# A fixed order by due times, w_in in four tiles, and weights loaded into lent places, in a convolution with two dense layers on one core

## The chip, the core and the metric

The kernel runs on one core of one Trainium2 chip. The engines of the core that matter here are TensorE (PE, matrix products), VectorE (DVE), ScalarE (ACT, one function of one input), GpSimd (POOL) and SyncE (SP), whose queue issues the DMAs. Each engine works off its own instructions in the order in which the program lists them; a semaphore makes one wait for another. The metric is the device time of one execution in microseconds (us), as the median of several runs.

## The reference

There are 8192 tokens of width 192 (two sequences of 4096).

```
w   = softmax(weight_gen)                       # [8192, 8 heads, 7 taps]
x   = sum over 7 taps of w * x shifted          # each head weighs its 24 columns
h   = x @ w_in                                  # 192 -> 2048
P   = a0 + a1 h + a2 h^2 + a3 h^3
Q   = 1 + |b0| |h| + |b1| h^2
y   = (P / (Q + 1e-6)) @ w_out                  # 2048 -> 192
xn  = y / sqrt(mean(y^2) + 1e-6) * rms_g
g   = xn @ w_gate ;  val = xn @ w_val           # 192 -> 1536
out = (g * sigmoid(g) * val) @ w_out2           # 1536 -> 192
```

## The kernel before

**Blocks.** The tokens go through in 32 blocks of 256. A block has four quarters of its 2048 hidden columns, numbered on through the program (block b has quarters 4b to 4b+3; below, .0 to .3 stand for the four of the block that a sentence is about). A step is a "job": a key, an engine, a cost, what it depends on and which places it takes.

The jobs of a block, with the lines of their instructions:
- convolution: `v` (POOL, L349), seven products of a shifted x with its weights; `a` (DVE L358, two reductions; POOL additions in the first blocks); `hl` (ACT L368) and `ll` (POOL L372) split the sum into two fp16 parts; `xt` transposes them by DMA (SP L377). `s` is the softmax in seven steps, of which `mx` (DVE L306) is the first.
- `mm1` of a quarter (PE L738): 20 matmuls into a place `h` in PSUM, of which there are two. So an mm1 waits until the quarter two before it has gone through its last reader, `d`.
- the rational function of a quarter, on tiles of 128x1024: `sq` (ACT L748) and `ab` (ACT L752), then `q` (DVE L755, the denominator), `ln` and `ex` (ACT L759, L762: one over it), `p1` and `p2` (DVE L766, L770: the numerator, in place in h), `hi` (DVE L775: the quotient in fp16, g1h), `qc` (ACT L778), `m` (POOL L781: denominator times g1h), `d` (DVE L784: what that leaves of the numerator) and `lo` (POOL L788: the low part, g1l).
- `mm2` (PE L804 to L806) into one PSUM place acc; `y`, `sj`, `rm` (ACT), the root `rn` (POOL L831 to L835, five small steps), `xs_` and `xh` (ACT L839, L843), `xl` (POOL L847, two instructions), `xnt` (SP L852: a transpose by DMA that gives xnT).
- `mm3` (PE L738 on gv): products with the gate and the value weights in two halves; `silu` (ACT), `prod` (DVE L883), `mm4` (PE L892) and the store.

**Weights.** They come as float64. An `ld` job loads a group of pieces as pairs of 32-bit words into a place `raw` (two of them) by SP. Three jobs decode it: `da` (ACT L409 to L412), `db` (DVE L431, L437, L440, L443: passes over the bits) and `dc` (ACT L455: squares and their sum). A list MODES gives each group its way of decoding: mode 0 has one pass more on DVE, mode 2 two instructions more on ACT per piece. From a maximum of the sums a scale is taken (`sc`), and `sa` and `sb` split each weight into a high and a low fp16 part (w1A, w1B, w1C for w_in; wo1h and wo1l for w_out; w3g.. and w3v.. for gate and value). The keys are in, o1, g, v and o2. The last pieces of w_in are copied to their place by DMA (L555).

**Order.** Before anything is emitted, a function `order()` simulates the engines and lists the jobs. Among the jobs of an engine whose inputs are ready it takes, at each moment of that simulation, the one that is due first. A job of block b is due at 4b times T_SLOT plus a number in a table OFF for its kind.

## Time and profile before

| | before |
|---|---|
| median of 3 runs | 1434.73 us (1432.48 to 1434.94) |
| profiled execution | 1432.05 us |
| its span in the profile | 1430.3 us |
| mean granted clock of PE | 0.957 of full speed |
| busy share of the span | PE 87%, DVE 82%, ACT 80%, POOL 73% |

All times of rows are of this one profiled execution. Its own time has 1.75 us outside the span. The profile's first part gives each engine's busy time over the whole span; a view by windows does so for stretches. A view of waits says for whom an engine stood idle, and for how long; a timeline lists single instructions with, in brackets, the idle time just ahead of one and what ended it.

### The profile page before, as it was taken

To read this page: it belongs to the slowest core of one execution; us is meant where nothing else is said; L and a number is where in the kernel's file an instruction comes from. 1 tells how busy PE (TensorE), PEld (TensorE's weight loads), DVE (VectorE), ACT (ScalarE), POOL (GpSimd) and SP (SyncE) were. 2 spreads that over 40 slices of the span, in tenths; PEclk is the share of its full clock that TensorE was granted. 3 is DMA by queue.
4 is the path that set the end of the run, shared out by engine and by line. 5 is a ranking of instruction groups with operands and counts; after the bars stand their busy time and mean duration, and the time that the engine had idled before them with its cause. 6 is when DMAs were issued, how large, how long until landed. Compare 5 with 4: busy or idle time off the path is not lost.

```text
span 1430.3 us, 26378 instructions
## 1 busy us (share of the span) xinstructions
PE 1240.0 (87%) x11026; PEld 1131.7 (79%) x11026; DVE 1174.0 (82%) x1021; ACT 1145.3 (80%) x1404; POOL 1041.2 (73%) x877
## 2 busy tenths in 40 slices
...
DMA packets 70376, 54.19 MB, mean 38 GB/s; under 512 B 54002, under 2 KB 65906, under 8 KB 69360
## 3 DMA queue, kind: packets, MB, share of 16 engines
...
q14 instruction: 34, 0.28, 0.1%
...
## 4 chain that ended last, share of the span: by engine, by line
PE 50%; POOL 17%; DVE 10%; ACT 10%; DMA 9%; issue 5%; SPq 0%; POOLq 0%; ACTq 0%; DVEq 0%
PE gv L738 19%; PE h L738 11%; PE acc L892 8%; POOL g1l L788 6%; DMA xnT<-xn 5%; PE acc L804 4%; PE acc L806 4%; PE acc L805 4%; POOL xn L847 4%; POOL tA L781 3%; DMA raw<-in_moe_w_in_dram 2%; DVE ac L358 2%; ACT L1285 1%; DVE tA L755 1%; DVE tA L784 1%
## 5 line engine op out<-in xcount | busy, mean ns | idle before, releaser
L781 POOL TENSOR_TENSOR tA<-tA,g1h 128x1024 f32<-128x1024 f32 x128 | 276.7, 2163 | 162.6 <-DVE g1h L775 146.7
L788 POOL TENSOR_TENSOR g1l<-tA,tC 128x1024 f16<-128x1024 f32 x128 | 305.7, 2400 | 105.4 <-DVE tA L784 62.8
L738 PE MATMUL h<-xt,w1A 128*128 128x256 f16 x1024 | 221.0, 279 | 78.0 <-DVE tA L784 76.5
L892 PE MATMUL acc<-wo,gp 128*128 128x192 f32 x1488 | 253.1, 326 | 0.6 <-ACT osb L898 0.5
L804 PE MATMUL acc<-wo1h,g1h 128*128 128x192 f16 x1024 | 251.9, 246 | 1.1 <-ACT y L811 1.1
L806 PE MATMUL acc<-wo1h,g1l 128*128 128x192 f16 x1024 | 251.9, 246 | 0.0
L805 PE MATMUL acc<-wo1l,g1h 128*128 128x192 f16 x1024 | 251.9, 246 | 0.0
L892 PEld LDWEIGHTS acc<-wo,gp 128*128 128x128 f32 x1488 | 240.3, 190 | 2.2 <-ACT osb L898 0.8
L349 POOL TENSOR_TENSOR pt<-xc,wg 128x384 f32<-128x384 f32 x224 | 240.3, 1089 | 1.0
L766 DVE SCALAR_TENSOR_TENSOR h<-tB,cf,h 128x1024 f32<-128x1024 f32 x128 | 164.0, 1281 | 87.0 <-ACT tA L752 87.0
L748 ACT ACTIVATE tB<-h 128x1024 f32<-128x1024 f32 x128 | 130.5, 1021 | 130.4 <-PE h L738 130.4
L784 DVE SCALAR_TENSOR_TENSOR tA<-h,cf,tA 128x1024 f32<-128x1024 f32 x128 | 164.0, 1281 | 63.0 <-POOL tA L781 62.9
L738 PE MATMUL h<-xt,w1C 128*128 128x256 f16 x1024 | 200.4, 278 | 0.0
L755 DVE SCALAR_TENSOR_TENSOR tA<-tB,cf,tA 128x1024 f32<-128x1024 f32 x128 | 188.4, 1472 | 0.5 <-ACT tB L748 0.4
L738 PEld LDWEIGHTS <-w1A 128*128 128x128 f16 x1024 | 102.2, 100 | 103.3 <-DVE tA L784 64.0
L738 PE MATMUL gv<-xnT,w3gA 128*128 128x256 f16 x756 | 157.2, 272 | 30.6 <-DMA xnT<-xn 30.5
L738 PE MATMUL gv<-xnT,w3vA 128*128 128x256 f16 x768 | 169.5, 273 | 3.3 <-ACT gp L878 3.3
L775 DVE SCALAR_TENSOR_TENSOR g1h<-h,cf,tC 128x1024 f16<-128x1024 f32 x128 | 163.7, 1279 | 8.6 <-ACT tC L762 3.4
L770 DVE SCALAR_TENSOR_TENSOR h<-tB,cf,h 128x1024 f32<-128x1024 f32 x128 | 163.6, 1278 | 0.0
L883 DVE SCALAR_TENSOR_TENSOR gp<-gp,val_s,gv 128x1536 f32<-128x1536 f32 x64 | 115.8, 1809 | 51.2 <-PE gv L738 51.2
L759 ACT ACTIVATE tC<-tA,cf 128x1024 f32<-128x1024 f32 x128 | 145.9, 1141 | 1.4 <-DVE tA L755 1.0
L762 ACT ACTIVATE tC<-tC,lnb 128x1024 f32<-128x1024 f32 x128 | 145.8, 1139 | 1.0
...
## 6 DMA issues: line engine op xcount, KB each, us to landing
...
```

What stands on the lines that cost most here:

```text
L349: nc.gpsimd.tensor_tensor(out=pt_t[b][:, k].rearrange("p i (h g) -> p i h g", h=NH), in0=xc_t[k0][:, o0 + k:o0 + k + 2, :].rearrange("p i ...
L738: nc.tensor.matmul(out=dst, lhsT=w[:, fs], rhs=xt[:, :, c, :], start=(n == 0), stop=(n == 4))
L755: nc.vector.scalar_tensor_tensor(out=tA[q], in0=tB[q], scalar=cfb(q)[:, 1:2], in1=tA[q], op0=ALU.mult, op1=ALU.add)
L766: nc.vector.scalar_tensor_tensor(out=h, in0=tB[q], scalar=cf[:, 4:5], in1=h, op0=ALU.add, op1=ALU.mult)
L775: nc.vector.scalar_tensor_tensor(out=g1h[q], in0=hps[q], scalar=cf[:, 3:4], in1=tC[q], op0=ALU.add, op1=ALU.mult)
L781: nc.gpsimd.tensor_tensor(out=tA[q], in0=tA[q], in1=g1h[q], op=ALU.mult)
L784: nc.vector.scalar_tensor_tensor(out=tA[q], in0=hps[q], scalar=cfb(q)[:, 3:4], in1=tA[q], op0=ALU.add, op1=ALU.subtract)
L788: nc.gpsimd.tensor_tensor(out=g1l[q], in0=tA[q], in1=tC[q], op=ALU.mult)
L804: nc.tensor.matmul(out=acc[:, 0:D], lhsT=g1h[q][:, r, ts], rhs=wo1h[:, f, :], start=(f == 0), stop=False)
L805: nc.tensor.matmul(out=acc[:, 0:D], lhsT=g1h[q][:, r, ts], rhs=wo1l[:, f, :], start=False, stop=False)
L806: nc.tensor.matmul(out=acc[:, 0:D], lhsT=g1l[q][:, r, ts], rhs=wo1h[:, f, :], start=False, stop=(f == N1 - 1))
L892: nc.tensor.matmul(out=acc[:, 0:D], lhsT=gp[b, k][:, i // 2, i % 2, ts], rhs=wo2[:, f, :], start=(f == 0), stop=(f == N2 - 1))
```

## The change

1. *The order.* `order()` no longer picks among what is ready. It works out a due time for each job: from a table TIMES for the weights and for blocks 0 to 11 (EARLY = 12), and from there on T_SLOT (now 9.8432) times the quarter plus OFF, which now has separate numbers for even and odd blocks. Each engine gets its jobs sorted by these, after they are raised where a dependence or a place demands it. The simulation that follows only picks between acc and h for a product's place. The costs in the jobs are changed (`over`, SYNC), and some dependences are added: the second half of y, sj and st behind the first, and `sa` of the value weights behind all `sb` of the gate.
2. *w_in in four tiles.* w1A, w1B and w1C are lists with a tile for each quarter of a block. The first four mm1 each wait only for the units of w_in that they read (W1_OF), where they had waited for all. Two of the copied pieces now span tiles: ten DMAs for eight.
3. *Lent places.* The raw words of the third w_out group, and of the last gate and value groups, go to `rawX`, which is memory of the later weight wo2; those of the fourth w_out group to `rawY`, which is w3vC. The decoded gate weights go to w3vA, w3vB and half of w3vC. So their loads need not wait for one of the two places `raw`.
4. *Modes.* The last two groups of w_in are decoded in mode 2 like the others.
5. *The column sums of w_in* use a matrix of ones. The rg2 matrices, scaled by rms_g on POOL (L502), are gone.

```diff
-MODES = [2, 2, 2, 2, 2, 2, 2, 2, 2, 2, 2, 2, 2, 2, 2, 0, 0, 1, 1, 1, 6, ...
+MODES = [2, 2, 2, 2, 2, 2, 2, 2, 2, 2, 2, 2, 2, 2, 2, 2, 2, 1, 1, 1, 6, ...
...
-    w1A = wts.tile([128, F1], FP16, name="w1A")
-    w1B = wts.tile([128, F1], FP16, name="w1B")
-    w1C = wts.tile([128, 2, F1], FP16, name="w1C")
+    FQ = F1 // QPB
+    w1A = [wts.tile([128, FQ], FP16, name=f"w1A{i}") for i in range(QPB)]
+    w1B = [wts.tile([128, FQ], FP16, name=f"w1B{i}") for i in range(QPB)]
+    w1C = [wts.tile([128, 2, FQ], FP16, name=f"w1C{i}") for i in range(QPB)]
...
+        over = dict(V=0.08, A=0.1, P=0.04).get(eng, 0.0)
+        cost, lat = max(0.1, cost - over), lat + over
...
+    def lent(which):
+        t = wo2.rearrange("p k f -> p (k f)")[:, 0:1536] if which == "rawX" else w3["v", "C"].rearrange("p a b -> p (a b)")
+        return t.bitcast(U32).rearrange("p (f t) -> p f t", t=2)
+
+    def lent_dec(i):
+        t = (w3["v", "A"], w3["v", "B"], w3["v", "C"][:, 0])[i]
+        return t.bitcast(FP32)
...
-                nc.tensor.matmul(out=cs[:, 0:width], lhsT=rg2[0], rhs=sq, ...
+                nc.tensor.matmul(out=cs[:, 0:width], lhsT=ones, rhs=sq, ...
...
-        for i in range(2):
-            nc.gpsimd.tensor_scalar(out=rg2[i], in0=rg2[i], scalar1=rg[:, i:i + 1], scalar2=rg[:, i:i + 1],
-                                    op0=ALU.mult, op1=ALU.mult)
...
         for q in (0, 1):
-            for p in (0, 64):
-                nc.sync.dma_start(out=W[2][p:p + 64, :, o[q]:o[q] + n], in_=hl[64 * q:64 * q + 64, :, 0:n])
+            a = 0
+            for c, m in wcols(W, 2, o[q], n):
+                for p in (0, 64):
+                    nc.sync.dma_start(out=c[p:p + 64], in_=hl[64 * q:64 * q + 64, :, a:a + m])
+                a += m
...
+                rt = {("o1", 2): "rawX", ("o1", 3): "rawY", ("g", 2): "rawX", ("v", 2): "rawX"}.get((nm, p[0]), "raw")
...
-    T_SLOT = 10.355
-    OFF = dict(da=[12.58, -130.43, -32.09, -74.27, -2.51], db=[-22.7, 19.98, 44.35, 145.62, 138.87], ...
+    T_SLOT = 9.8432
+    EARLY = 12
+    OFF = dict(wg=([-44.46], [0]), s=([-9.28, -9.78, -2.06, 1.81, 4.88, -28.84, 70.96], [0, 0, 0, 0, 0, 0, 0]),
...
+    TIMES = [5.35, 6.66, -7.44, 14.88, 0.19, 12.86, 24.5, 26.36, 28.9, -28.42, 25.15, 32.13, 34.55, 38.07, 33.34, 27.63,
...
+    W1_OF = [(0,), (1,), (1, 2), (1, 2, 3)]
...
-        job(("mm1", q), "T", 2.19, lambda q=q: mm1(q), [("xt", b)] + (w_done["in"] if q < 4 else []), new=[h], use=[x])
+        job(("mm1", q), "T", 2.19, lambda q=q: mm1(q), [("xt", b)] + ([w_done["in"][k] for k in W1_OF[q]] if q < 4 else []), ...
...
-    SYNC, SWITCH, NEAR = 0.12, 1.3, 3.0
+    SYNC, SWITCH = 0.15, 1.3
...
+        times, want = iter(TIMES), []
+        for k in keys:
+            p = place(k)
+            if p is None or p[2] is None or J[k]["due"] is not None or p[2] < EARLY * QPB:
+                want.append(next(times))
             else:
...
+                want.append(T_SLOT * p[2] + OFF[p[0]][p[2] // QPB % 2][p[1]])
...
+        queue = {e: [i for i in seq if J[keys[i]]["eng"] == e] for e in "SNTVAP"}
```

What this moves, first on DVE in the loop: from the first product of block 16 to its second, in which quarters .0 and .1 of block 18 end (the numbers in names are tiles). Before, `q.0 hi.1 p1.0 a p2.0 d.1 hi.0 a mx d.0`:

```order
L883 SCALAR_TENSOR_TENSOR gp_8556<-gp_8556,val_s_137,gv_99 128x1536
L755 SCALAR_TENSOR_TENSOR tA_8652<-tB_8635,cf1_128,tA_8652 128x1024
L775 SCALAR_TENSOR_TENSOR g1h_8724<-h_8561,cf1_128,tC_8667 128x1024
L766 SCALAR_TENSOR_TENSOR h_8599<-tB_8635,cf1_128,h_8599 128x1024
L358 TENSOR_REDUCE ac_8753<-pt_8477 128x192
L770 SCALAR_TENSOR_TENSOR h_8599<-tB_8635,cf1_128,h_8599 128x1024
L784 SCALAR_TENSOR_TENSOR tA_8622<-h_8561,cf1_128,tA_8622 128x1024
L775 SCALAR_TENSOR_TENSOR g1h_8809<-h_8599,cf1_128,tC_8726 128x1024
L358 TENSOR_REDUCE ac_8753<-pt_8477 128x192
L306 TENSOR_REDUCE mx_8846<-wg_8695 128x32
L784 SCALAR_TENSOR_TENSOR tA_8652<-h_8599,cf1_128,tA_8652 128x1024
L883 SCALAR_TENSOR_TENSOR gp_8782<-gp_8782,val_s_137,gv_99 128x1536
```

Now the same stretch, where the lines are L784 for q, L795 and L799 for p1 and p2, L804 for hi, L361 for a, L813 for d and L912 for the product:

```order
L912 SCALAR_TENSOR_TENSOR gp_8537<-gp_8537,val_s_145,gv_99 128x1536
L784 SCALAR_TENSOR_TENSOR tA_8652<-tB_8625,cf1_136,tA_8652 128x1024
L795 SCALAR_TENSOR_TENSOR h_8604<-tB_8625,cf1_136,h_8604 128x1024
L804 SCALAR_TENSOR_TENSOR g1h_8779<-h_8562,cf1_136,tC_8666 128x1024
L361 TENSOR_REDUCE ac_8794<-pt_8539 128x192
L813 SCALAR_TENSOR_TENSOR tA_8599<-h_8562,cf1_136,tA_8599 128x1024
L799 SCALAR_TENSOR_TENSOR h_8604<-tB_8625,cf1_136,h_8604 128x1024
L804 SCALAR_TENSOR_TENSOR g1h_8804<-h_8604,cf1_136,tC_8671 128x1024
L361 TENSOR_REDUCE ac_8794<-pt_8539 128x192
L813 SCALAR_TENSOR_TENSOR tA_8652<-h_8604,cf1_136,tA_8652 128x1024
L912 SCALAR_TENSOR_TENSOR gp_8801<-gp_8801,val_s_145,gv_99 128x1536
```

The first d of the stretch moved ahead of p2; the step mx of the softmax moved out of it. In odd blocks the order is now `q.0 hi.1 a d.1 p1.0 p2.0 hi.0 a d.0`, with d ahead of both p1 and p2, and a q stands right behind the second product too. On POOL `lo.1 m.0 rn lo.0 xl` stays as it is, and the products v.2 to v.6 of a block stand together, where v.2 and v.3 stood between the m's and lo's of the other two quarters.

Second, ACT in the head, where w_in has been decoded (L455 is the last dc of w_in; L476 and L478 are its sa; L409 to L412 the da of the third w_out group). Before, hl of the first block (L368) is ahead of them:

```order
L455 ACTIVATE sq,mx8o_140<-dec 128x768
L368 ACTIVATE hl<-ac 128x2x192
L476 ACTIVATE w1A<-wdec,s_in 128x512
L478 ACTIVATE wdec<-wdec,s_in 128x512
L476 ACTIVATE pk<-wdec,s_in 128x512
L478 ACTIVATE wdec<-wdec,s_in 128x512
L409 ACTIVATE sq<-raw 128x768
L411 ACTIVATE sq<-sq,thr 128x768
L412 ACTIVATE sq<-sq 128x768
L455 ACTIVATE sq,mx8o_140<-dec 128x768
```

Now (hl is L371, the da starts with L423):

```order
L490 ACTIVATE w1A_101<-wdec,s_in 128x512
L492 ACTIVATE wdec<-wdec,s_in 128x512
L490 ACTIVATE pk<-wdec,s_in 128x512
L492 ACTIVATE wdec<-wdec,s_in 128x512
L423 ACTIVATE sq<-wo_120 128x768
L425 ACTIVATE sq<-sq,thr 128x768
L426 ACTIVATE sq<-sq 128x768
L469 ACTIVATE sq,mx8o_148<-dec 128x768
L371 ACTIVATE hl<-ac 128x2x192
```

hl moved behind the split of that part of w_in and behind da and a dc of w_out.

Third, SP in the head, from the small parameters on. Before, the last w_out load (L574) stands behind the copies of w_in (L555) and the first transpose (L377):

```order
L574 DMA raw<-in_moe_w_out_dram 128x4x384 x3
L192 DMA wg<-in_weight_gen_dram 128x224
L555 DMA w1C<-pk 64x2x512 x4
L377 DMA_TRANSPOSE xt<-hl 128x6x128
L574 DMA raw<-in_moe_w_out_dram 128x4x384
```

Now (w_out's load is L601; wo_120 is memory of wo2, and w3vC that of a value weight):

```order
L601 DMA raw<-in_moe_w_out_dram 128x4x384
L601 DMA wo_120<-in_moe_w_out_dram 128x4x384
L601 DMA w3vC<-in_moe_w_out_dram 128x4x384
L195 DMA wg<-in_weight_gen_dram 128x224
```

The third and the fourth load moved up behind the second, ahead of all copies.

## Rows read from the trace of the kernel before

**Rows 1.** The page's part 1: busy time, share of the span, instructions.
```profile
PE 1240.0 (87%) x11026; PEld 1131.7 (79%) x11026; DVE 1174.0 (82%) x1021; ACT 1145.3 (80%) x1404; POOL 1041.2 (73%) x877
```

**Rows 2.** Windows: stretch, length, busy by engine, PEclk, DMA share, GB/s.
```profile
core 0: us, PE busy (x) PEld busy (x) DVE busy (x) ACT busy (x) POOL busy (x), PEclk, DMA share, GB/s
90.00:200.00 110.00, 40.98 (x324) 33.56 (x325) 103.85 (x102) 78.86 (x99) 84.22 (x53) 0.66 0.28 73
303.00:1345.00 1042.00, 1002.05 (x9056) 924.37 (x9056) 888.53 (x687) 881.75 (x1064) 791.26 (x663) 1.00 0.09 24
1345.00:1431.00 86.00, 79.22 (x690) 73.36 (x688) 33.53 (x25) 42.55 (x58) 21.99 (x22) 1.00 0.05 13
```

**Rows 3.** PE's waits, 303 to 1345 us: us, times, longest.
```profile
PE gv L738 <- DMA xnT<-xn: 28.3, 27, 2.0
PE h L738 <- DVE tA L784: 10.2, 26, 0.8
```

**Rows 4.** Timeline of DVE in the loop: start, us, instruction, [idle before <- releaser].
```profile
795.05 1.81 DVE L883 SCALAR_TENSOR_TENSOR gp<-gp,val_s,gv 128x1536 f32<-128x1536 f32 x1 [0.60 <-PE gv L738]
...
834.50 1.81 DVE L883 SCALAR_TENSOR_TENSOR gp<-gp,val_s,gv 128x1536 f32<-128x1536 f32 x1 [0.24 <-PE gv L738]
...
839.81 2.54 DVE L358 TENSOR_REDUCE ac<-pt 128x192 f32<-128x1344 f32 x1
...
843.43 1.30 DVE L784 SCALAR_TENSOR_TENSOR tA<-h,cf,tA 128x1024 f32<-128x1024 f32 x1
844.62 1.30 DVE L775 SCALAR_TENSOR_TENSOR g1h<-h,cf,tC 128x1024 f16<-128x1024 f32 x1
...
849.37 1.28 DVE L784 SCALAR_TENSOR_TENSOR tA<-h,cf,tA 128x1024 f32<-128x1024 f32 x1 [0.73 <-POOL tA L781]
```

**Rows 5.** Timeline of POOL in the loop.
```profile
813.65 2.03 POOL L847 TENSOR_TENSOR xn<-y,xn 128x256 f16<-128x256 f32 x2
...
818.80 1.06 POOL L372 TENSOR_TENSOR hl<-ac,hl 128x256 f16<-128x256 f32 x2
...
830.28 3.50 POOL L349 TENSOR_TENSOR pt<-xc,wg 128x384 f32<-128x384 f32 x3
...
844.87 2.37 POOL L788 TENSOR_TENSOR g1l<-tA,tC 128x1024 f16<-128x1024 f32 x1 [3.86 <-DVE tA L784]
847.19 2.14 POOL L781 TENSOR_TENSOR tA<-tA,g1h 128x1024 f32<-128x1024 f32 x1
```

**Rows 6.** Timeline of ACT and of SP's DMA queue in the loop.
```profile
850.85 0.80 ACT L839 ACTIVATE y<-y,r 128x192 f32<-128x192 f32 x2 [1.06 <-POOL r L835]
...
815.71 1.21 SPq L852 DMA_TRANSPOSE xnT<-xn  x1
```

**Rows 7.** DVE's waits, 10 to 200 us: us, times, longest.
```profile
DVE dec L431 <- ACT sq L412: 11.4, 4, 5.5
DVE wo1l L485 <- ACT wo1h L476: 3.8, 1, 3.8
```

**Rows 8.** Timeline of the head, rows of all engines.
```profile
12.47 0.72 ACT L411 ACTIVATE wdec<-wdec,thr 128x512 f32<-128x512 f32 x1
...
39.57 2.48 DVE L443 SCALAR_TENSOR_TENSOR wdec<-wdec 128x512 f32<-128x512 f32 x2
44.12 0.68 DVE L443 SCALAR_TENSOR_TENSOR wdec<-wdec 128x512 f32<-128x512 f32 x1
47.70 1.66 POOL L502 TENSOR_SCALAR rg<-rg,rg 128x128 f32<-128x128 f32 x2 [4.92 <-PE gv L458]
54.50 0.52 ACT L368 ACTIVATE hl<-ac 128x384 f16<-128x384 f32 x1 [5.58 <-POOL ac L364]
60.41 0.96 DVE L431 SCALAR_TENSOR_TENSOR dec<-raw,sq 128x768 uint32<-128x768 uint32 x1 [5.52 <-ACT sq L412]
63.21 0.51 SPq L574 DMA_DIRECT2D raw<-in_moe_w_out_dram  x1
67.89 0.89 ACT L409 ACTIVATE sq<-raw 128x768 f32<-128x768 f32 x1 [2.59 <-DMA raw<-in_moe_w_out_dram]
...
89.47 1.57 DVE L755 SCALAR_TENSOR_TENSOR tA<-tB,cf,tA 128x1024 f32<-128x1024 f32 x1 [0.36 <-ACT tB L748]
```

More of the change, by code (lines that the diff above doesn't have):

```diff
@@ L111 @@
     ident = const.tile([128, 128], FP32, name="ident")
-    rg2 = [wts.tile([128, 128], FP32, name=f"rg2_{i}") for i in range(2)]
+    ones = wts.tile([128, 128], FP32, name="ones")
     a_sb = const.tile([128, 4], FP32, name="a_sb")
@@ L529, with wcols, wcol @@
     pk = {}
+    def wcols(W, k, f0, n):
+        w, step = (W[k], FQ) if isinstance(W[k], list) else ([W[k]], F2)
+        while n:
+            i, a = divmod(f0, step)
+            m = min(n, step - a)
+            yield w[i][..., a:a + m], m
+            f0, n = f0 + m, n - m
+    def wcol(W, k, f0, n):
+        return next(wcols(W, k, f0, n))[0]
     def piece_a(nm, F, pc, W, s, aside=False):
@@ new lines, in order @@
+        keys = list(J)
+        n = len(keys)
+        num = {k: i for i, k in enumerate(keys)}
+        deps = [[num[d] for d in dict.fromkeys(J[k]["deps"])] for k in keys]
+        users, succ = {}, [[] for _ in keys]
+        for i, k in enumerate(keys):
+            for u in J[k]["new"] + J[k]["use"]:
+                users.setdefault(u, []).append(i)
+            for d in deps[i]:
+                succ[d].append(i)
+        left, topo = [len(d) for d in deps], []
+        st = [i for i in range(n) if not left[i]]
@@ new lines, in order, with free_at @@
+        queue = {e: [i for i in seq if J[keys[i]]["eng"] == e] for e in "SNTVAP"}
+        live, end, done = {r: [] for r in CAPS}, [0.0] * n, [False] * n
+        free, held, tab, mm1_left, out = dict.fromkeys("SNTVAP", 0.0), dict(P=(0.0, 0.0), V=(0.0, 0.0)), "e", NQ, []
+        def free_at(r):
+            l = live[r]
+            if len(l) < CAPS[r]:
+                return 0.0
+            w = users[l[len(l) - CAPS[r]]]
+            return max(end[x] for x in w) if all(done[x] for x in w) else None
```

308 lines of the change are left out of this document (130 added, 178 removed), and 116 rows, old and new, of the table TIMES.

## The prediction

> **What bounds the kernel now.** I read the busy shares first, then the same by stretch, then the waits of the busiest engine, then the rows of one block. TensorE (PE) is busy for 1240.0 us, 87% of the span [rows 1]. That is an average over stages, and the stretches part them [rows 2]: from 303 to 1345 us PE works 1002.05 of 1042 us at a granted clock of 1.00 and no other engine over 889; from 90 to 200 us it works 40.98 of 110, and VectorE (DVE) 103.85. So there are three stages: a head that DVE limits, a long loop that PE limits, and a tail of 86 us in which PE works 79.22.
>
> In the loop PE waits for two things and for nothing else [rows 3]: xnT, the transposed input of the gate products, 28.3 us in 27 waits, and d (DVE's L784), whose end frees the PSUM place of the next mm1, 10.2 us in 26. Together 38.5 us. The loop turns once in 39.45 us (the product of one block at 795.05, that of the next at 834.50 [rows 4]), so 1042 us are 26.4 blocks and each loses 38.5 / 26.4 = 1.46 us. PE alone would need 38.0.
>
> Why xnT is late is followed back from there. Its transpose is issued at 815.71 [rows 6], when xl has ended (813.65 + 2.03) [rows 5]. Ahead of xl stand on GpSimd (POOL), here with the times of the next turn: lo.1 from 844.87, m.0 from 847.19 [rows 5], the small steps of the root, and lo.0. They follow each other without a gap, and lo.1 had waited 3.86 us for d.1. DVE ends d.1 at 844.73, since five others stand between the product and it, the reduction a (2.54) among them [rows 4]. The other input of m.0 is hi.0, which ends at 845.92 [rows 4]. So m.0 starts 1.27 us after its inputs are there, only because lo.1, released late, is in its way. DVE then waits 0.73 for m.0 ahead of d.0 [rows 4].
>
> **The change part by part: the loop.** In the new order d.1 stands ahead of p2.0 (even blocks) or of p1.0 and p2.0 (odd blocks), and so 1.2 or 2.4 us earlier, a pass being 1.2 from start to start [rows 4]. In an even block it ends at 843.5; lo.1 (2.37) is done by 845.9, as hi.0 ends at its old time 845.92, for the number of passes ahead of hi.0 is the same. m.0 starts at about 846.05 instead of 847.19. The steps behind it have no gap, so all move with it, and xnT with them: 1.14 us for even blocks. I take 1.04 for odd ones, where the reduction comes a place sooner and the row of passes behind it ends a tenth later. d.0 moves too, and with it the wait of mm1. A turn then loses 1.46 - 1.1 = 0.4 us and lasts 38.4. What is next late is PE itself at 38.0, then ScalarE's xs_, which already waits 1.06 for the root [rows 6] and moves along.
>
> How many blocks gain: 12 to 30 have the new order as a rule, 19 blocks; of the blocks below 12, whose order is a table of times, 5, 6, 8 and 9 have d.1 early, and 4, 7, 10 and 11 have not. I take 24, half of each kind: 12 x 1.14 + 12 x 1.04 = 26.2 us. Bounds: 18 (19 blocks, a little under one us each) and the whole 38.5 of [rows 3].
>
> The products v of the convolution move on POOL: two of them stood among the m's and lo's of the other two quarters, now five stand together behind those. They cost nothing as long as the last ends before DVE comes to the reduction; the 3.86 us that POOL waits in front of lo.1 [rows 5] are the cover. What they cost without it is a rival below. The extra order between the halves of y, sj and st is the one in which ScalarE does them anyway: 0.
>
> **The head.** What DVE gets done earlier ahead of 90 us shifts all that follows, as it has 6 us of air in 110 [rows 2]. The change takes off DVE's line:
> - Two last groups of w_in are decoded in three DVE passes instead of four. The dropped passes are 2.48 (two pieces) and 0.68 [rows 8]: 3.16 us. ScalarE gets six more instructions for it; one on a piece of 512 took 0.72 [rows 8], so some 4 us. ScalarE stood idle for 5.58 us in this stretch, ahead of hl [rows 8], so I cost them at 0. Without that cover they would eat the gain.
> - At 60.41 DVE waits 5.52 us for ScalarE, which at 54.50 had stood 5.58 behind hl of the first block, waiting for POOL [rows 8]. In the new order hl stands behind the split of w_in and the first steps of the next weights: 5.52 goes. POOL is also rid of two multiplications (1.66) for which it waited 4.92 for PE [rows 8], which brings hl itself nearer.
> - The load of the fourth w_out group is issued only at 63.21, behind copies and a transpose on SP's queue, and ScalarE waits 2.59 for it at 67.89 [rows 8], DVE behind it. It now goes to a place lent by a weight that comes later and stands near the front of the queue: 2.59 goes. The two more copies of w_in pieces on that queue, at 0.51 an issue, stand behind it: 0.
> - The wait of DVE's wo1l for ScalarE, 3.8 us [rows 7], stays: ScalarE now has the gate weights' decoding ahead of that step.
>
> Sum: 3.16 + 5.52 + 2.59 = 11.3 us. Below: only the passes come off and the waits turn up elsewhere, 3. Above: all 11.4 us that DVE's decoding waits for ScalarE [rows 7] and the passes, 14.6. I take 11.3, since each of its terms has a row of its own. A w_in tile for each quarter lets mm1 of the first quarters begin before the last piece is split; what that gives is inside this sum, for q follows on DVE, the limit.
>
> **The tail.** The new order sets the last block's gate product ahead of an mm4 that had covered the wait for its xnT. PE idles 7 us of 86 there [rows 2]; some 2 come in and some 2 go: 0 +/- 2.
>
> **Sum.** 11.3 + 26.2 = 37.5 us. The profiled execution took 1432.05 us (span 1430.3): 1394.6. The median of the runs is 2.7 above it, and with that the forecast is **1397 us**.
>
> **The rivals.**
> 1. *Only the head gains.* d.1 goes up, but xnT is held at its old time by something else, for instance the root, which needs ScalarE's sums of y. Against it: ScalarE waits 1.06 for POOL there [rows 6], not POOL for ScalarE. 1434.7 - 11.3 = 1423.
> 2. *Only the loop gains.* The weights come no earlier, because SP's queue, served in order, stands behind the first load that waits for its place, or because the lent places are waited for. For it: the load at 63.21 [rows 8] was late for such a reason. 1434.7 - 26.2 = 1408.
> 3. *xl is locked out by q.* xl took 2.03 us here; a pair of the same shape took 1.06 [rows 5]. In odd blocks q is now the first pass after the block's second product, so it can start just ahead of xl. If xl then waits for a whole pass of 1.28 [rows 4], it takes 1.28 + 1.06 = 2.34 us, 0.31 more: 12 odd blocks x 0.31 = 3.7 us less gain, 1401. The Trainium skill, page "SBUF — State Buffer", section "Who interferes with whom", says that a DVE instruction with two SBUF inputs contends with a GpSimd instruction that reads SBUF, and that the shared port pair is an exclusive lock for whoever issues first. By that rule q locks the first half of xl out too (1401); by the row it costs xl one us, as it does already (1397). The pair 2.03 against 1.06 agrees with the rule, and no row shows q ahead of the whole xl.
> 4. *Slower: five products in a row.* They must end before DVE's reduction a, which stands ahead of d.1 and hi.0. Three took 3.50 us from 830.28 [rows 5], 1.17 each; with two fewer ahead, the five begin at 828.0. In an odd block a is third after the product (834.50 + 1.7 + 2 x 1.2 = 838.6), so there are 10.6 us for 5.8 us of work. From 2.1 us each on they delay a, and the loop one for one; at 2.33 an odd block gains nothing. At 2.6 (13.0 us) odd blocks lose 2.4 - 1.04 = 1.4 and even ones, where a is one place later, 0.1: 12 x 1.5 = 18 us, less 11.3 from the head: 1441. Against it: more than twice the price in the row.
> 5. *It doesn't do what it says:* the waits of head and loop only change their names, 1435.
>
> **How the numbers follow.** A measurement of this kernel can tell about 0.2% (3 us) from no change. Chances: forecast 0.50 (its own range 1383 to 1411), rival 3 0.08, rival 1 0.15, rival 2 0.15, rival 4 0.08, rival 5 0.04. Faster: 0.50 + 0.08 + 0.15 + 0.15 = 0.88; same 0.04; slower 0.08. The low end has both upper bounds and the tail, 1434.7 - 14.6 - 38.5 - 2 = 1380, and 4 more for like waits in the blocks before 303 us: 1376. The high end takes in rival 2 and about half of rival 1: 1424. What is left out is about 0.2.
>
> **What would show it.** Right: a turn of 38.4 us; PE's waits for xnT and d in the loop near 10 us in place of 38.5; lo.1 done before hi.0 ends, m.0 within 0.15 of that end, and DVE without its wait ahead of d.0; in the head no wait of 5 us of DVE's decoding for ScalarE, the first q at about 80 us instead of 89.47 [rows 8], and PE busy throughout 11 us earlier. Wrong: PE's waits for xnT as long as before although m.0 is earlier (then the root or xl is late); DVE's a waiting for the products; DVE still standing for a load at 60 to 70 us; a first q at 86 or later, which would say that only the passes were gained.

## The result, and the profile after

| | before | changed kernel |
|---|---|---|
| median | 1433.61 us (4 runs, 1432.28 to 1434.94) | 1414.15 us (4 runs, 1409.12 to 1416.43) |
| ratio of the times | | 0.986, 95% interval 0.983 to 0.989 |
| profiled execution, its span | 1432.05, 1430.3 us | 1413.59, 1411.8 us |

The change made the kernel 19.5 us faster, 1.4%. The forecast was 37.5 us, so it had the direction and about twice the size: 1414 lies outside the range of the forecast itself (1383 to 1411) and inside the outer range (1376 to 1424), between the times of rivals 2 and 1.

The page's first part, the changed kernel. PE's work is the same as in [rows 1] (1240.0); DVE has three passes fewer and is busy 27 us longer:

```profile
PE 1241.5 (88%) x11026; PEld 1134.7 (80%) x11026; DVE 1200.8 (85%) x1018; ACT 1153.9 (82%) x1410; POOL 1044.7 (74%) x874
```

The windows that answer to [rows 2] (stretch, length, busy by engine, PEclk, DMA share, GB/s), the loop's end moved with the span. In the loop PE idles 26 of 1022 us where it idled 40 of 1042:

```profile
90.00:200.00 110.00, 52.47 (x414) 42.73 (x415) 106.85 (x100) 82.34 (x102) 88.33 (x57) 0.73 0.25 66
303.00:1325.00 1022.00, 995.97 (x9028) 922.05 (x9026) 901.66 (x683) 882.80 (x1060) 787.32 (x661) 1.00 0.10 24
1325.00:1412.00 87.00, 80.75 (x708) 75.00 (x705) 35.70 (x26) 43.39 (x59) 24.30 (x23) 1.00 0.05 12
```

PE's waits in the loop, 303 to 1325 us (us, times, longest). Both waits of [rows 3] are about halved, in number and in sum, and two new ones stand under them:

```profile
PE gv L767 <- DMA xnT<-xn: 14.9, 16, 1.6
PE h L767 <- DVE tA L813: 5.3, 11, 0.8
PE gv L767 <- ACT gp L907: 3.0, 11, 0.9
PE gv L767 <- DVE gp L912: 2.7, 9, 0.7
```

Most of the single waits that are left are as long as before, for the loop now **alternates**. From one block's first gate matmul to the next block's it takes 37.9 us when the next block is odd and 40.0 when it is even, over 14 turns in a row (blocks 13 to 26), where every turn took 39.5 before. Two first gate matmuls of the timeline of PE, blocks 16 and 17, the second without a wait:

```profile
809.19 0.27 PE L767 MATMUL gv<-xnT,w3gA 128*128 128x256 f16 x1 [1.03 <-DMA xnT<-xn]
...
847.15 0.27 PE L767 MATMUL gv<-xnT,w3gA 128*128 128x256 f16 x1
```

What makes the difference is seen on POOL, which prepares that transpose. The first row is xl ahead of the long wait, the second xl ahead of none; before, every xl of the loop took 2.03 to 2.05 (one of them in [rows 5]):

```profile
804.31 2.04 POOL L876 TENSOR_TENSOR xn<-y,xn 128x256 f16<-128x256 f32 x2
...
842.95 1.04 POOL L876 TENSOR_TENSOR xn<-y,xn 128x256 f16<-128x256 f32 x2
```

And on DVE at the same moments (L784 is q, L795 is p1). Behind the one product stands q, behind the other p1:

```profile
802.11 1.81 DVE L912 SCALAR_TENSOR_TENSOR gp<-gp,val_s,gv 128x1536 f32<-128x1536 f32 x1 [0.28 <-PE gv L767]
803.84 1.59 DVE L784 SCALAR_TENSOR_TENSOR tA<-tB,cf,tA 128x1024 f32<-128x1024 f32 x1
...
841.28 1.81 DVE L912 SCALAR_TENSOR_TENSOR gp<-gp,val_s,gv 128x1536 f32<-128x1536 f32 x1 [0.81 <-PE gv L767]
843.01 1.28 DVE L795 SCALAR_TENSOR_TENSOR h<-tB,cf,h 128x1024 f32<-128x1024 f32 x1
```

In the loop's turns of all the kernels below, xl costs one us more wherever a q starts up to 0.56 us behind its start or runs already; where the next q came 0.65 us behind or later, it cost nothing. In the long turns PE waits for xnT just that one us.

**Where the 18.5 us of the span came from.** I compare the starts of first gate matmuls. Block 3 is 3.5 us earlier than before (301.53 for 305.01), block 12 7.2, block 30 18.0. So head 3.5, blocks 3 to 12 3.7, blocks 12 to 30 10.9, rest 0.5. The forecast had 11.3 for the head and 26.2 for the loop. The head's share is that of one execution: in the profiles of this kernel and of six below that differ from it only from block 12 on, block 3 starts anywhere from 296.5 to 303.6, and in three with the head of before from 305.0 to 305.4. So the head's gain at block 3 is 1 to 9 us, and never the 11.3. From block 3 to block 12 the same seven take 350.9 to 352.7 us, against 355.6 before.

### The profile page after: what moved, and what is told of

It is laid out like the page before. It is cut to its first block, busy times and chain, and to the rows that moved or that the text cites. A ratio compares the mean times of both kernels' runs of the same rounds, so it can differ in the third digit from the quotient of the medians.

```text
span 1411.8 us, 26479 instructions
## 1 busy us (share of the span) xinstructions
PE 1241.5 (88%) x11026; PEld 1134.7 (80%) x11026; DVE 1200.8 (85%) x1018; ACT 1153.9 (82%) x1410; POOL 1044.7 (74%) x874
## 4 chain that ended last, share of the span: by engine, by line
PE 37%; DVE 16%; ACT 14%; POOL 13%; issue 5%; DMA 4%; POOLq 0%; DVEq 0%; ACTq 0%
PE gv L767 15%; PE h L767 9%; PE acc L921 6%; POOL g1l L817 6%; DMA xnT<-xn 4%; DVE tA L784 3%; DVE g1h L804 3%; DVE h L799 3%; POOL tA L810 3%; POOL xn L876 2%; DVE gp L912 2%; ACT tC L791 2%; ACT tC L788 2%; ACT tA L807 2%; PE acc L835 2%
## 5 line engine op out<-in xcount | busy, mean ns | idle before, releaser
L833 PE MATMUL acc<-wo1h,g1h 128*128 128x192 f16 x1008 | 248.0, 246 | 0.4 <-ACT y L840 0.4
L834 PE MATMUL acc<-wo1l,g1h 128*128 128x192 f16 x1008 | 248.0, 246 | 0.0
L835 PE MATMUL acc<-wo1h,g1l 128*128 128x192 f16 x1008 | 248.0, 246 | 0.0
L921 PEld LDWEIGHTS acc<-wo,gp 128*128 128x128 f32 x1464 | 236.8, 191 | 3.0 <-ACT osb L927 1.7
L784 DVE SCALAR_TENSOR_TENSOR tA<-tB,cf,tA 128x1024 f32<-128x1024 f32 x128 | 201.8, 1577 | 32.9 <-ACT tA L781 32.9
L813 DVE SCALAR_TENSOR_TENSOR tA<-h,cf,tA 128x1024 f32<-128x1024 f32 x128 | 163.7, 1279 | 41.8 <-POOL tA L810 41.8
L767 PE MATMUL gv<-xnT,w3gA 128*128 128x256 f16 x756 | 164.7, 275 | 33.1 <-DMA xnT<-xn 29.1
L795 DVE SCALAR_TENSOR_TENSOR h<-tB,cf,h 128x1024 f32<-128x1024 f32 x128 | 163.5, 1279 | 34.4 <-ACT tA L781 31.3
L804 DVE SCALAR_TENSOR_TENSOR g1h<-h,cf,tC 128x1024 f16<-128x1024 f32 x128 | 163.6, 1278 | 12.0 <-ACT tC L791 3.4
L781 ACT ACTIVATE tA<-h,cf 128x1024 f32<-128x1024 f32 x128 | 142.0, 1110 | 35.2 <-PE h L767 19.1
L799 DVE SCALAR_TENSOR_TENSOR h<-tB,cf,h 128x1024 f32<-128x1024 f32 x128 | 163.9, 1281 | 1.3
L912 DVE SCALAR_TENSOR_TENSOR gp<-gp,val_s,gv 128x1536 f32<-128x1536 f32 x64 | 115.8, 1810 | 51.5 <-PE gv L767 51.0
```

The lines of the kernel that those rows point to most:

```text
L767: nc.tensor.matmul(out=dst, lhsT=w[:, fs], rhs=xt[:, :, c, :], start=(n == 0), stop=(n == 4))
L784: nc.vector.scalar_tensor_tensor(out=tA[q], in0=tB[q], scalar=cfb(q)[:, 1:2], in1=tA[q], op0=ALU.mult, op1=ALU.add)
L799: nc.vector.scalar_tensor_tensor(out=h, in0=tB[q], scalar=cf[:, 5:6], in1=h, op0=ALU.mult, op1=ALU.add)
L804: nc.vector.scalar_tensor_tensor(out=g1h[q], in0=hps[q], scalar=cf[:, 3:4], in1=tC[q], op0=ALU.add, op1=ALU.mult)
L833: nc.tensor.matmul(out=acc[:, 0:D], lhsT=g1h[q][:, r, ts], rhs=wo1h[:, f, :], start=(f == 0), stop=False)
L834: nc.tensor.matmul(out=acc[:, 0:D], lhsT=g1h[q][:, r, ts], rhs=wo1l[:, f, :], start=False, stop=False)
```

## The experiments

Three theories stood against each other. *PE next:* with d.1 early the loop is PE's, as the prediction had it. *Lockout:* xl beside q sets xnT. *Sum of DVE or POOL:* the order of other steps holds the loop. Times of kernels with the changed head spread by up to 9 us from run to run (1407 to 1416), so of these the lengths of turns in the profile say more than the medians. The table has all kernels, means of turns that end at blocks 13 to 26; "product" is the time from the first gate matmul to the start of the first product.

| kernel | median us | short turn / long turn | xl, short / long | PE's wait for xnT, long | product, long | q.0, long |
|---|---|---|---|---|---|---|
| before | 1434 | 39.5 / 39.5 | 2.04 / 2.04 | 1.01 | 16.0 | 1.28 |
| changed | 1414.2 | 37.9 / 40.0 | 1.05 / 2.04 | 1.02 | 17.1 | 1.42 |
| before_d1 | 1392.7 | 37.9 / 37.7 | 1.06 / 1.06 | 0.00 | 16.0 | 1.28 |
| before_d1_q2 | 1414.3 | 38.9 / 38.7 | 2.04 / 2.05 | 0.93 | 16.0 | 1.28 |
| after_even | 1410.6 | 37.9 / 39.9 | 1.06 / 2.05 | 0.95 | 17.2 | 1.42 |
| after_odd | 1414.9 | 37.9 / 40.1 | 1.06 / 2.04 | 1.03 | 17.2 | 1.42 |
| after_p1out | 1413.9 | 37.9 / 39.9 | 1.06 / 2.04 | 1.02 | 16.9 | 1.42 |
| after_q2 | 1412.4 | 38.5 / 39.3 | 1.06 / 1.06 | 0.04 | 17.4 | 1.43 |
| after_s | 1412.4 | 37.9 / 40.2 | 1.06 / 2.04 | 1.02 | 16.8 | 1.80 |
| after_s_q2 | 1413.4 | 37.9 / 40.2 | 1.06 / 2.04 | 1.03 | 16.8 | 1.80 |
| after_row | 1409.4 | 37.9 / 39.5 | 1.06 / 2.04 | 1.02 | 16.3 | 1.80 |
| after_best | 1411.0 | 37.9 / 40.0 | 1.06 / 2.04 | 1.02 | 16.5 | 1.81 |
| after_modes | 1413.3 | 37.9 / 39.8 | 1.06 / 2.04 | 1.03 | 16.9 | 1.42 |
| after_x2 | 1412.6 | 37.9 / 40.0 | 1.06 / 2.04 | 1.02 | 17.1 | 1.42 |

### The kernel before with one step moved

```diff
+        todo = order()
+        for q in range(25, NQ, 4):
+            n = [t[0] for t in todo]
+            i, j = n.index(("p2", q - 1)), n.index(("d", q))
+            if i < j:
+                todo.insert(j, todo.pop(i))
-        for k, res in order():
+        for k, res in todo:
```

> The kernel before with one edit: from block 6 on p2.0 is put behind d.1, so DVE does q.0 hi.1 p1.0 a d.1 p2.0 hi.0; nothing else moves on any engine. This is the loop's part of the prediction alone: 26 blocks x 1.1 = 28.6 us by the prediction, 1405; by the ring of 76.9 a turn is 38.45 instead of 39.47, 26.5 us, 1407. Rival (DVE is full and another order does not help): turns of 39.0 or more, 1422 or slower.

Measured: 1392.68 us, ratio 0.971 (0.970 to 0.973), 41 us off. One neighbouring pair on one engine does twice what the whole change does. PE's waits in the loop, 303 to 1305 us:

```profile
PE gv L738 <- DMA xnT<-xn: 3.0, 2, 2.0
PE h L738 <- DVE tA L784: 0.6, 1, 0.6
```

The window of the same stretch, where PE idles 4 of 1002 us:

```profile
303.00:1305.00 1002.00, 997.95 (x9075) 927.68 (x9074) 886.96 (x688) 884.78 (x1065) 797.26 (x664) 1.00 0.10 25
```

Both forecasts of it were too small, and POOL's timeline tells why:

```profile
861.98 2.37 POOL L788 TENSOR_TENSOR g1l<-tA,tC 128x1024 f16<-128x1024 f32 x1 [2.66 <-DVE tA L784]
864.57 2.14 POOL L781 TENSOR_TENSOR tA<-tA,g1h 128x1024 f32<-128x1024 f32 x1 [0.22 <-DVE g1h L775]
...
868.35 2.37 POOL L788 TENSOR_TENSOR g1l<-tA,tC 128x1024 f16<-128x1024 f32 x1 [0.16 <-DVE tA L784]
870.67 1.07 POOL L847 TENSOR_TENSOR xn<-y,xn 128x256 f16<-128x256 f32 x2
```

The block's product starts at 852.81 here. m.0 starts 11.76 behind it, against 847.19 - 834.50 = 12.69 before [rows 4, 5]: 0.93 earlier. xl starts 0.77 earlier, not 1.14, because hi.0 came 0.2 later and lo.0 waited 0.16 for d.0. But xl then **ends** 1.74 earlier, for it takes 1.07 instead of 2.05: its second instruction starts at 871.30, ahead of q.2 (871.55), so that q.2 no longer comes between the two. The 1.74 is more than the 1.46 that PE had waited.

### Is it the lockout?

The same kernel, and in each block q.2 put ahead of p1.2 behind the second product:

```diff
...
+        for q in range(26, NQ, 4):
+            n = [t[0] for t in todo]
+            i, j = n.index(("p1", q)), n.index(("q", q))
+            if i < j:
+                todo.insert(j, todo.pop(i))
```

> The kernel before with d.1 ahead of p2.0 (as in before_d1), and then q.2 ahead of p1.2 from block 6 on. In before_d1 xl takes 1.07 us, since it runs beside the product and p1.2 and is done when q.2 starts, and xnT arrives just as PE is done with its other work (turn 37.8). Theory (xl is locked out): with q.2 first, xl takes 2.04, xnT is 1.0 us later and every turn 38.8, so 1393 + 26 x 1.0 = 1419 us. Rival (what before_d1 gained is d.1 alone): turns of 37.8 to 38.0 as before, 1393 to 1398.

Measured: 1414.32 us, 21.6 above before_d1, with turns of 38.9 and 38.7 as the lockout has it. DVE's and POOL's rows of the timeline, q.2 and xl of one block:

```profile
882.82 1.45 DVE L755 SCALAR_TENSOR_TENSOR tA<-tB,cf,tA 128x1024 f32<-128x1024 f32 x1
...
883.14 2.05 POOL L847 TENSOR_TENSOR xn<-y,xn 128x256 f16<-128x256 f32 x2
```

And PE's waits from 303 to 1325 us:

```profile
PE gv L738 <- DMA xnT<-xn: 26.9, 27, 2.0
```

The swap adds no work and takes none away. xl stands 1.0 longer and PE waits 1.0 longer, in 25 turns. That the lockout of xl by q is worth one us a turn is shown by this pair. It also parts before_d1's gain: of its 41 us some 20 are d.1's own (before to before_d1_q2, turns of 39.5 to 38.8), and 21.6 are the lockout that went with it (38.8 to 37.8). The Trainium skill says ("SBUF — State Buffer", "Who interferes with whom") that a DVE instruction with two SBUF inputs contends with a GpSimd instruction that reads SBUF. The traces agree: of DVE's passes in the loop only q has both of its tile inputs in SBUF, and only q has longer and shorter rows (1.27 to 2.22 us in the changed kernel, where the other passes of its size take 1.26 to 1.30).

### Why the changed kernel keeps its long turns

First its two orders of d.1, exchanged one for the other.

```diff
-  p1=([126.96, ...], [138.35, ...]), p2=([135.87, ...], [133.48, ...
+  p1=([126.96, ...], [128.8, ...]), p2=([135.87, ...], [138.36, ...      (after_even)
+  p1=([135.2, ...], [138.35, ...]), p2=([135.87, ...], [133.48, ...      (after_odd)
```

> The changed kernel with one edit: from block 12 on the odd blocks take the even blocks' order of DVE passes (q.0 p1.0 hi.1 a d.1 p2.0 hi.0). Theory (two-turn ring): the loop alternates between a turn of 37.9 us without a wait and one of about 40.0, because the odd order brings xnT only 0.55 us nearer and the even order 1.8, and the surplus of the even turn is lost where PE has no air. With the even order everywhere a ring of two turns is 32.1 (PE, first gate matmul to second product) + 23.1 (DVE, second product to the next first product) + 21.7 (first product to xnT) = 76.9, so every turn is 38.4 to 38.5 and the kernel takes 1414 - 19 x 0.5 = 1404 us. Rival (DVE is simply full): no turn under 39.0, 1414.

> The changed kernel with one edit: from block 12 on the even blocks take the odd blocks' order (q.0 hi.1 a d.1 p1.0 p2.0 hi.0). Theory (two-turn ring): each ring of two turns is 32.1 + 23.1 + 22.9 = 78.1 as it is now, so all turns are 39.0 and the time stays at 1414 us within 3. Rival (each turn gains for itself what its order gives, even 1.5 and odd nothing): all turns as long as the present long ones, 40.0, and 1414 + 10 x 2 = 1434 us.

Measured: 1410.56 and 1414.91 us, and the long turn stays where it was (39.9, 40.1). So the ring as I wrote it fell: which of the two orders a block has is not what makes its turn long. The 1414 us forecast for after_odd came, but not its turns of 39.0. Next, one pass less on DVE: p1 of each block's quarter .1 is left out, and with it a part of the numerator.

```diff
-        job(("p1", q), "V", 1.28, lambda q=q: dve_p1(q), ...
+        job(("p1", q), "V", 1.28, lambda q=q: None if q % 4 == 1 and q > 48 else dve_p1(q), ...
```

> The changed kernel without p1 of each block's quarter .1 from block 12 on: a part of the numerator is left out there, and one DVE pass of 1.2 us in the stretch from a block's second product to the next block's first product. Theory (two-turn ring with DVE's 23.1 us stretch in it): the stretch becomes 21.9, the ring 76.8 instead of 78.0, and the time 1414 - 10 x 1.2 = 1402 us. Rival (the loop waits only for POOL's row lo.1, m.0, root, lo.0, xl): the pass is beside the point and the time stays at 1414.

Measured: 1413.88 us, long turns 39.9; the 1402 did not come. DVE's sum of work is not it either. Then the swap that cost 21.6 us above, the other way round:

```diff
...
+        for q in range(54, NQ, 8):
+            n = [t[0] for t in todo]
+            i, j = n.index(("q", q)), n.index(("p1", q))
+            if i < j:
+                todo.insert(i, todo.pop(j))
```

> The changed kernel with one edit: in odd blocks from 13 on, p1.2 goes ahead of q.2 on DVE (one neighbouring pair changes places). Theory (xl is locked out): in the odd turns q.2 runs beside xl, which takes 2.04 us, while in the even turns, where p1.2 is first, it takes 1.05; with p1.2 first everywhere xl takes 1.05, the odd turns go from 39.9 to 38.9, and the time from 1414 to 1414 - 9 x 1.0 = 1405 us. Rival (xl's length does not matter, the odd turn is long because its first product is 1.3 us late): xl may be shorter, but the odd turns stay within 0.3 of 39.9, 1411 to 1414.

Measured: 1412.42 us. The lockout is gone (xl 1.06 in all turns) and so is PE's wait for xnT (0.04), and still the mean turn is 38.9 as it was: the long one lost 0.7 and the short one gained 0.6. PE's waits from 303 to 1325 us show what took the place:

```profile
PE h L767 <- DVE tA L813: 10.4, 21, 1.0
PE gv L767 <- DMA xnT<-xn: 5.8, 7, 1.5
```

PE now waits for d, 10.4 instead of 5.3 us. My reading then, which the next runs were to test, was that there are two things to take away, each hiding the other. The second is the late first product (17.1 instead of 16.0 in the long turn), which waits on DVE's line: in the changed kernel the reciprocal of the softmax stands there and waits for POOL, and q behind it runs 1.72 beside POOL:

```profile
861.27 0.35 DVE L332 RECIPROCAL sm<-sm 128x32 f32<-128x32 f32 x1 [0.27 <-POOL sm L328]
861.54 1.72 DVE L784 SCALAR_TENSOR_TENSOR tA<-tB,cf,tA 128x1024 f32<-128x1024 f32 x1
863.18 1.27 DVE L799 SCALAR_TENSOR_TENSOR h<-tB,cf,h 128x1024 f32<-128x1024 f32 x1
864.37 1.80 DVE L912 SCALAR_TENSOR_TENSOR gp<-gp,val_s,gv 128x1536 f32<-128x1536 f32 x1
```

So I moved the two small steps, alone and with the swap (from block 12 on):

```diff
...
+        def put(k, l, off=1):
+            e = todo.pop([t[0] for t in todo].index(k))
+            todo.insert([t[0] for t in todo].index(l) + off, e)
+        for b_ in range(12, NBLK - 2, 2):
+            c_ = blk_chunk[b_][0] + 2
+            if ("s", c_, 0) in J:
+                put(("s", c_, 0), ("a", b_ + 1, 1))
+                put(("s", c_, 5), ("a", b_ + 2, 1))
+        for q_ in range(54, NQ, 8):                    (after_s_q2 only)
+            put(("p1", q_), ("q", q_), 0)
```

> The changed kernel, from block 12 on, with two small DVE steps of the softmax moved: the maximum s.0 from between q.2 and p2.2 back to behind the second reduction, and the reciprocal s.5 from ahead of q.5 to behind the next block's second reduction, where the kernel before has them. Theory (two causes in the long turns): in the turns of the profile in which no softmax is left (the last two long ones) the long turn is 38.75 instead of 40.0, so the softmax steps cost 1.2; the rest, 0.9, is PE's wait for xnT, which xl's lockout by q.2 makes. So long turns of 38.8 and 1414 - 8 x 1.2 = 1404 us. Rival (the long turn is long for DVE's sum of work, which stays): 1414.

> As after_s, and also p1.2 ahead of q.2 in odd blocks from 13 on (as after_q2, which alone gave 2 us at most). Theory (two causes, each hides the other): with both gone no turn is long, 37.9 throughout, and the time is 1414 - 8 x 2.1 - 2 x 0.9 = 1395 us, 9 below after_s. Rival (after_q2's result holds here too): the same as after_s within 2 us.

Measured: 1412.38 and 1413.40 us, long turns 40.2 in both, where 1404 and 1395 us had been expected. The product came 0.4 earlier, but q.0 behind it grew from 1.42 to 1.80, and with the swap xl is locked out again: xl itself came so late that q.2 overtook it with p1.2 ahead (q.2 starts 0.36 us behind xl's start). So two causes that hide each other are not shown. The same moves in blocks 5 to 11 with the moved load of below:

> As after_s_q2, and the same moves in blocks 5 to 11 (s.0 and s.5 from block 8 on, p1.2 ahead of q.2 from block 5 on, p2.0 behind d.1 in blocks 7, 10 and 11), and the load x.2 behind the first store as in after_x2. Theory: PE idles 7.9 us in the turns that end at blocks 5 to 11, of which some 5 go, and x.2 gives 1 to 4: 1395 - 5 - 2 = 1388 us, below before_d1's 1393. Rival (those early turns wait for something else, or the head's lowered clock eats it): 1393 to 1395.

Measured: 1411.01 us; long turns 40.0; the 1388 did not come. Last, DVE's whole order of before_d1 from block 6 on, the other engines as they were but for the moved load of below:

```diff
...
+        put(("x", 2), ("out", 0))
...
+            row += [("prod", b_ - 2, 0, 0), q_("q", 0), q_("hi", 1), q_("p1", 0), ("a", b_ + 1, 0), q_("d", 1), q_("p2", 0),
+                    q_("hi", 0), ("a", b_ + 1, 1), ..., q_("d", 0),
+                    ("prod", b_ - 2, 1, 0), q_("p1", 2), q_("q", 2), q_("p2", 2), q_("q", 3), q_("p1", 3), q_("hi", 2),
+                    q_("p2", 3), q_("hi", 3), q_("d", 2)] + ([] if j_ else [("s", c_, 3)]) + [
+                    q_("d", 3), q_("p1", 5), q_("q", 5), q_("p2", 5)]
...
+        lines["V"] = [(next(new), "acc") if t[0] in left else t for t in lines["V"]]
```

> The changed kernel with DVE's whole order of before_d1 from block 6 to 29 (q.0 hi.1 p1.0 a d.1 p2.0 hi.0 a s d.0, product, p1.2 q.2 p2.2 q.3 p1.3 hi.2 p2.3 hi.3 d.2 s.3 d.3 p1.5 q.5 p2.5), all other engines in their order, and the load x.2 behind the first store as in after_x2. Theory (several places of DVE's order hold the loop at once, so that one alone gives nothing): the turns that end at blocks 7 to 30 last 37.8 to 38.0, which takes out the 22 us that PE idles in them now, and x.2 gives 2: 1390 us. Rival (POOL's order holds it, the five products in a row and ll behind two of them): with DVE's order of before_d1 the long turns stay at 39 or more, 1405 us or more.

Measured: 1409.36 us, long turns 39.5, as the rival had it. The same row of passes on DVE that runs a turn in 37.7 in before_d1 needs 39.5 here, so what holds it stands on another engine, and the product is nearly on time (16.3). POOL's and DVE's rows of a long turn:

```profile
858.06 4.15 POOL L352 TENSOR_TENSOR pt<-xc,wg 128x384 f32<-128x384 f32 x5
...
859.75 1.81 DVE L912 SCALAR_TENSOR_TENSOR gp<-gp,val_s,gv 128x1536 f32<-128x1536 f32 x1 [0.64 <-PE gv L767]
861.49 1.80 DVE L784 SCALAR_TENSOR_TENSOR tA<-tB,cf,tA 128x1024 f32<-128x1024 f32 x1
...
878.13 2.04 POOL L876 TENSOR_TENSOR xn<-y,xn 128x256 f16<-128x256 f32 x2
...
878.50 1.40 DVE L784 SCALAR_TENSOR_TENSOR tA<-tB,cf,tA 128x1024 f32<-128x1024 f32 x1
```

The five products in a row end at 862.21, while q.0 runs; it takes 1.80 instead of 1.28. All behind it is half a us late, xl starts 0.37 ahead of q.2 instead of 0.9, and that half us costs a whole one. In the same kernel one turn to an even block, the one to block 28, has no softmax steps ahead of the products on POOL; there they end 0.18 us behind the start of q.0, q.0 takes 1.28, xl 1.06, and the turn lasts 37.8. The turn behind it lasts 38.5 instead of 37.9, so that some 0.6 of the 1.7 come back:

```profile
1243.70 5.13 POOL L352 TENSOR_TENSOR pt<-xc,wg 128x384 f32<-128x384 f32 x5
...
1246.92 1.81 DVE L912 SCALAR_TENSOR_TENSOR gp<-gp,val_s,gv 128x1536 f32<-128x1536 f32 x1
1248.65 1.28 DVE L784 SCALAR_TENSOR_TENSOR tA<-tB,cf,tA 128x1024 f32<-128x1024 f32 x1
```

That is what the trace offers as the cause of the 1.6 us left in the long turns: the five products together on POOL with a softmax step of 1.33 us ahead of them (in the turn to block 28 they are together too, and without the step they do no harm). In before_d1 the step is there as well, but with three products behind it, which end ahead of q.0. A kernel with the products back between the m's and lo's was not run, so it stays argued and not shown.

### The head

```diff
-MODES = [2, 2, 2, 2, 2, 2, 2, 2, 2, 2, 2, 2, 2, 2, 2, 2, 2, 1, ...
+MODES = [2, 2, 2, 2, 2, 2, 2, 2, 2, 2, 2, 2, 2, 2, 2, 0, 0, 1, ...
...
+            if k in (("db", ("in", (4, 5)), 4), ("db", ("in", (6,)), 4)):
+                want.append(want[-1] + 0.01)
+                continue
```

> The changed kernel with the last two groups of w_in decoded in four DVE passes again (MODES 0), all else in the same order. The prediction's term: two passes of 2.48 and 0.68 come back ahead of the first q, 3.2 us, and the whole kernel is 3.2 us longer, 1417. Rival (ScalarE or the loads are what the head waits for there, and the passes were covered): the first q moves by less than 1 us and the time stays at 1414.

Measured: 1413.27 us, where 1417 had been expected; but 3 us are less than these kernels spread. The first q starts 2.95 later, as the term had it (85.20 for 82.25; 81.2 to 82.4 in the six others with the same head). The d that PE waited for at the head's end is 0.4 later than in the changed kernel's profile (177.01 for 176.61), but 1.0 to 3.1 later than in the six others (173.9 to 176.0). So the two passes are real time at 82 us; whether they still are at 177 and at the end stays open.

The second look is at block 1. In the changed kernel PE waits 3.98 us for its xnT, which [rows 3]'s stretch does not show and no early block of the kernel before had. On SP's queue a load of 1344 KB (and one of 384 KB behind it) stands ahead of the transpose, which then took 6.5 us to land, against 2.8 in the loop:

```profile
207.96 0.58 SPq L183 DMA_DIRECT2D xc<-in_x_dram  x1
209.47 0.33 SPq L217 DMA_DIRECT2D xp<-in_x_dram  x1
211.15 1.55 SPq L881 DMA_TRANSPOSE xnT<-xn  x1
...
217.68 0.34 PE L767 MATMUL gv<-xnT,w3gA 128*128 128x256 f16 x1 [3.98 <-DMA xnT<-xn]
```

The load of 1344 KB alone was moved:

```diff
+        todo = order()
+        n = [t[0] for t in todo]
+        todo.insert(n.index(("out", 0)), todo.pop(n.index(("x", 2))))
```

> The changed kernel with one edit: on SP's queue the load x.2 (1344 KB) stands behind the first store instead of just ahead of the transpose xnt.1. Theory: the 6.5 us that this transpose took, against 2.8 in the kernel before, are the load's doing, and PE's wait of 3.98 us at the first gate matmul of block 1 goes: xnT lands 2.8 us after its issue and the time is 1414 - 3.7 = 1410. Rival (DVE limits there anyway): the wait of PE goes and comes back within two blocks, 1413 to 1415.

Measured: 1412.61 us. The wait is gone: PE's waits for xnT from 190 to 303 us, first the changed kernel, then this one:

```profile
PE gv L767 <- DMA xnT<-xn: 5.0, 2, 4.0
```

```profile
PE gv L767 <- DMA xnT<-xn: 1.3, 2, 1.0
```

In the eight profiles with the load ahead of the transpose block 1's wait is 2.9 to 4.8 us, in the three with it moved at most 0.3. PE's granted clock is 1.00 now in the two windows of 10 us in which it had been 0.89 and 0.94. The changed kernel, then this one:

```profile
210.00:220.00 10.00, 6.02 (x39) 5.05 (x38) 9.96 (x6) 6.37 (x6) 7.84 (x8) 0.89 0.71 184
220.00:230.00 10.00, 10.00 (x70) 9.46 (x70) 6.50 (x8) 6.38 (x6) 6.25 (x5) 0.94 0.00 0
```

```profile
210.00:220.00 10.00, 8.95 (x63) 8.00 (x62) 9.96 (x7) 8.14 (x9) 6.39 (x6) 1.00 0.13 31
220.00:230.00 10.00, 9.16 (x79) 8.16 (x77) 6.82 (x8) 6.09 (x7) 9.82 (x7) 1.00 0.19 54
```

Block 1 begins 5.4 us earlier than in the changed kernel, block 3 only 3.0, of which 1.7 were there at block 0. So of 3.7 expected some 1.3 seem to arrive, but block 3 varies by 7 us from run to run with the same head, and neither that nor the medians can tell. The load's guilt at the wait is shown; what the whole kernel has of it is not.

## Why the prediction was right, and where it missed

- *What bounds the kernel:* right. The loop is PE's, and nearly all of its 38.5 us of waits can be had: before_d1 leaves 3.6 of them.
- *d.1 moves m.0 forward:* right in kind. In the changed kernel lo.1 is done (796.82) before hi.0 is (798.21), m.0 starts 0.17 behind that, and DVE's wait ahead of d.0 is gone:

```profile
794.45 2.37 POOL L817 TENSOR_TENSOR g1l<-tA,tC 128x1024 f16<-128x1024 f32 x1 [1.49 <-DVE tA L813]
798.38 2.13 POOL L810 TENSOR_TENSOR tA<-tA,g1h 128x1024 f32<-128x1024 f32 x1 [1.56 <-DVE g1h L804]
```

But hi.0 did not keep its old time. It ends 11.91 us behind the product here and 11.65 in the turn behind, where it ended 11.42 behind it before. So m.0 is 0.6 (odd block) and 0.9 us (even block) nearer to the product, and not 1.04 and 1.14.

- *All behind m.0 has no gap and moves by as much, 1.14 and 1.04:* **the step that failed**, in both directions. xl is not a fixed 2.03. It is 1.05 or 2.04, by where q stands. Where it fell free (before_d1, the short turns) xl ended 1.6 to 1.9 us earlier; in the long turns of the changed kernel xl ends 20.05 behind the product (786.30 to 806.35), 0.6 earlier than the 20.67 before.
- *What is next late is PE at 38.0:* wrong for every second turn. What was next late was xl beside q, and the first product, 1.1 us later. Ahead of that stand the softmax's reciprocal and a q that runs beside POOL; moving the softmax's two steps (after_s) brought the product 0.4 nearer, and what the rest is was not parted. DVE's first product had waited for PE only 0.24 [rows 4]; that row was the warning, and I did not price what a DVE line without air does when steps are added to it. Mean turn 38.95 instead of 38.4, and the table's blocks 3 to 12 gained 3.7 in nine turns: 14.6 us for the loop instead of 26.2.
- *The five products cost nothing (rival 4):* they did not delay the reduction (DVE has no wait for them from 303 to 1325 us), and at 0.85 to 1.92 each, 1.09 on the mean, the price was near that in [rows 5]. But they reach into q.0. The place was right; the mechanism, as far as it is argued above, was another.
- *xl is locked out by q (rival 3):* the mechanism was right and its price too small. I took the 2.03 of [rows 5] as the state without lockout and asked for 0.31 more. The pair of 1.06 in the same rows was the true one. In the kernel before, q.2 had started 0.36 us behind each xl of the loop, here behind that of [rows 5] at 813.65:

```profile
814.01 1.39 DVE L755 SCALAR_TENSOR_TENSOR tA<-tB,cf,tA 128x1024 f32<-128x1024 f32 x1
```

So the lockout had cost about 1.0 us a turn all along (the price of the pair before_d1 and before_d1_q2), two thirds of what PE waited.

- *The head:* its sum of 11.3 came close where it was made, and was not kept. The waits of 5 us of DVE's decoding for ScalarE went; from 10 to 200 us, where [rows 7] had 11.4:

```profile
DVE dec L445 <- ACT sq L426: 1.5, 2, 1.1
```

DVE's waits for loads of x grew by 3.0 in the same stretch (8.6 for 5.6). The first q came 7.2 us earlier and PE's 400th matmul 9.9 earlier (193.1 for 203.0). Then 6.4 us were given back before block 3 in this execution: 4.3 more in waits (block 1's xnT, 3.98, is the largest) and 2.1 in a longer busy time of PE, whose granted clock was lower for a part of it. The prediction followed the gain to the end of DVE's limit and took it as kept: that is the second step that failed. Of its terms only the 3.16 of the two passes was put to a run of its own, which left open what they are worth behind 82 us; the lent places and the four tiles of w_in were not tested alone.

- *The tail:* 0 was right, 0.5.
